# Reciprocal of the attention denominators by ln and exp on ACT, and a new order of the late units

## The chip, the cores and the metric

The kernel runs on one core of a Trainium2 chip. The metric is the device time of one execution in microseconds (us). Engines are named as in the profile: PE (matrix multiply; PEld is its weight load), DVE (vector), ACT (activation functions and copies), POOL (general), SP (which here issues all DMAs). A core has an on-chip memory, SBUF, and an accumulator memory, PSUM, into which PE writes.

## The reference

Two independent heads are computed and laid side by side in the output. S = 2048, D = 576, inputs in bf16.

```python
# A: a short convolution of k, times v, then a long convolution over the sequence (by FFT), times q
k_shift = sum over t of k_pad[:, t:t + S, :] * shift_k[:, ks - 1 - t]        # ks = 4
kv = k_shift * v
y = irfft2(rfft2(kv padded to 2S) * rfft2(ssm_k padded to 2S))[:, :S, :]
a = q * (y + kv * ssm_D)
# B: linear attention, H = 32 heads of 18
q, k, v = split(x @ wqkv)
phi = lambda t: where(t > 0, t + 1, exp(t)) + 1e-6
pq, pk = phi(q), phi(k)
kv = einsum("bhsd,bhse->bhde", pk, v);  z = einsum("bhsd->bhd", pk)
num = einsum("bhqd,bhde->bhqe", pq, kv)
den = einsum("bhqd,bhd->bhq", pq, z)[..., None] + 1e-6
b = (num / den) reshaped @ wo
out = concatenate([a, b], axis=-1)
```

## The kernel before

Part A computes the long convolution as a Fourier transform on PE, in five chunks of channels (four of 128, one of 64; chunk 4 is the small one). For each chunk ci: `cv` is the short convolution on DVE or POOL, four stages on the tile at, the last one times v; `h1` and `u1` are the first transform stage of the filter and of the data (eight matmuls of G, evicted to tiles Ch and Cu); `ht` and `ut` are DMA transposes of Ch and Cu, issued by SP, into Cth and Ctu; `h2` and `u2` are the second stage, evicted to T and SU, in two halves with two planes each; `pX`, `pT`, `pS` and `pA` are products and sums of SU and T in SBUF (an "N" in their place skips a sum, and the inverse transform then does one plane of matmuls more); `i1` is the first inverse stage, evicted to V; `i2` the second, whose eviction on DVE multiplies by q (L608). `st` stores.

Part B: `k`, `q` and `qt` make phi (an Exp on ACT, then DVE); `G`, `zs`, `zz`, `kv` and `M` make the matrix of the heads (V weights wv, x, then the output weights wo, joined into B['M'] in the tile wo_M) and the sums of pk; `den` makes the denominators of all positions and heads, 128 partitions x 512, in one PSUM tile den_ps, and their reciprocal rden, which lies in the tile Gz; `bc` (four chunks) and `bt` spread rden by matmuls over the channels, and DVE multiplies pqT and pq4 by it (L753, L762); `o` and `ol` multiply by M and store. No `o` can start before all `bc` and `bt` are done.

The order of all work is written out in a table of 296 units, ORDER, read from left to right; every engine executes its share in that order. A unit is a name with its arguments (chunk, half or plane), a letter for the engine (A ACT, D DVE, P POOL, N none), and behind the slash the places that it takes in rings of SBUF tiles and in PSUM. PSUM has four places, 0 to 3; a matmul group waits until the group that had its place before is evicted. Ch, Cu and V share two SBUF places (c8); the transposed tiles share two.

ACT holds the tables of a set of functions. The kernel loads one for the sines at the start and one for Exp in `_sine16`.

Of the kernel before, what the change touches and what calls it, by code (L numbers as in the profile page):

```python
# [42 lines left out]
h1.2.0.1.D/0 u2.1.1.1.A/03 zs/01 ut.1.0/1 u2.1.1.0.A/2 pA.0.0.N i1.0.0.0.D/10 i1.0.0.1.A/3 i1.0.1.0.A/1 zz/2
i1.0.1.1.A/0 pX.1.1.D/0 vl.1/0 cv.2.3.DDD ht.2.0/0 pT.1.1.D u2.1.0.1.A/13 u2.1.0.0.A/2 ht.2.1/1 FT.1.T hT.3.a/02 hd.4
G.3/1 cv.3.0.D cv.3.1.DD u1.2.0.0.A/00 lwv pS.1.1.D u1.2.1.1.A/3 G.0/2 cv.3.2.DD u1.2.1.0.A/1 pX.1.0.D/1 pA.1.0.N
u1.2.0.1.A/0 G.4/3 h2.2.1.1.A/22 cv.3.3.DDD h2.2.1.0.A/1 G.2/0 cv.4.0.D i2.0.0/3 h2.2.0.0.A/02 h2.2.0.1.A/1 wom kv/0
# [1 line left out]
i1.1.1.0.A/0 u2.2.0.1.A/3 pT.1.0.D cv.4.1.DD den/2 u2.2.1.1.A/11 pS.1.0.N i1.1.0.1.A/0 i1.1.0.0.A/3 lwo M.3.A/1 M.2.A/0
i2.1.1/3 u2.2.1.0.A/1 i2.1.0/0 ht.3.1/1 h2.3.1.1.A/12 hT.4.p/02 u1.3.1.1.A/01 bc.2/32 u1.3.0.1.A/0 u1.3.0.0.A/1 bt/3
M.1.A/0 u1.3.1.0.A/2 h2.3.1.0.D/1 ht.3.0/0 h2.3.0.1.A/33 bc.0/02 st.0 ut.3.0/1 h1.4.1.0.A/11 h1.4.0.1.A/3 h1.4.1.1.A/1  # L50
h2.3.0.0.A/0 bc.3/31 pX.2.0.P/0 pT.2.0.P M.4.A/2 ut.3.1/0 pX.2.1.P/1 h1.4.0.0.A/0 M.0.A/3 bc.1/20 pA.2.0.N pT.2.1.D
pS.2.1.D u2.3.0.0.A/01 u2.3.0.1.A/3 pS.2.0.P cv.4.2.PD cv.4.3.DDD i1.2.0.1.A/02 i1.2.0.0.A/1 ht.4.0/1 pX.3.0.D/0 ql.1/1
o.1.2.AAf/03 pA.2.1.P i1.2.1.1.A/2 o.0.2.AA/10 u1.4.0.0.D/13 i1.2.1.0.D/2 u1.4.1.0.A/1 h2.4.0.1.A/03 u1.4.1.1.D/0
u1.4.0.1.A/1 u2.3.1.1.A/12 u2.3.1.0.A/3 ut.4.0/0 pT.3.0.D h2.4.0.0.A/0 i2.2.1/1 pX.3.1.D/1 pA.3.1.D pS.3.0.D pA.3.0.P
o.1.0.AA/23 pT.3.1.D o.0.0.AAf/10 u2.4.0.0.A/02 u2.4.0.1.D/3 i1.3.0.1.A/11 i2.2.0/0 i1.3.0.0.A/2 st.1 pX.4.0.D/0
pT.4.0.D pA.4.0.D pS.3.1.P i1.3.1.0.A/3 pS.4.0.D i1.3.1.1.A/1 o.1.3.AAs/02 i2.3.0/3 i1.4.0.0.A/01 i1.4.0.1.D/0 i2.3.1/2
# [196 lines left out]
def kernel(  # L253
# [469 lines left out]
    def b_den():  # L723
        ps = psum.tile([128, 1024], FP32, name="den_ps")
        for c in range(4):
            for j in range(4):
# [12 lines left out]
        nc.vector.tensor_scalar_add(out=ez[:], in0=ps[:, 512:513], scalar1=EPS)
# [1 line left out]
        nc.vector.tensor_scalar(out=den, in0=den, scalar1=ez[:, 0:1], scalar2=None, op0=ALU.add)
        with nc.allow_low_precision(reason="the reciprocal is used as bf16"):
            nc.vector.reciprocal(out=B['rden'], in_=den)
# [151 lines left out]
```

## Time and profile before

| | |
|---|---|
| median of three runs | 158.18 us (158.04 to 158.29) |
| the profiled execution | 159.33 us, span of its instructions 157.6 us |
| mean granted PE clock | 0.989 |
| busy: PE, DVE, ACT, POOL | 149.6, 135.8, 130.5, 62.0 us |
| DVE's add of ez to den_ps, reciprocal of den_ps | 0.76 and 3.36 us |
| largest waits of PE in the trace | 1.1 (start), 0.5, 0.4, 0.4, 0.3 us |

How to read it: a row of a timeline gives start, duration, engine, line, operation, tile written and tiles read, how many instructions are merged, and in brackets the idle time of the engine before it and what ended that. A row of a group gives the busy total and the mean in ns of one instruction, then idle time before. In a table by stretches, "x" counts the instructions and PEclk is the share of PE's full clock that was granted. Times are us from the span's start.

### The profile page before, as it was taken

Reading aid. Unit: us, or ns where it says so; the run is one execution under the profiler, and the core shown is the slowest. Engines: PE = TensorE matmul, PEld = TensorE weight load, DVE = VectorE, ACT = ScalarE, POOL = GpSimd, SP = SyncE. Lnnn points to the kernel's source line nnn. Section 1 sums busy time; section 2 is a strip of 40 time slices with the busy share of each in tenths; the row PEclk is TensorE's granted clock in tenths of the full one; section 3 lists DMA queues with packets and bytes.
Section 4 is the critical chain, followed back from the end, with each engine's and each line's share of the span. In section 5 each row is a group of like instructions: output and inputs, shape, how many; then the busy total and the mean of one; then the engine's idle time right before and its main releaser. Section 6 shows DMA issues by size and latency. Waiting matters only on the chain.

```text
span 157.6 us, 4600 instructions
## 1 busy us (share of the span) xinstructions
PE 149.6 (95%) x1986; PEld 90.3 (57%) x1986; DVE 135.8 (86%) x169; ACT 130.5 (83%) x162; POOL 62.0 (39%) x70
## 2 busy tenths in 40 slices
PE   7999999999998999999999999999899999999991
PEld 2686555467533467367566468585445565578650
DVE  6989779898999699997999998999998998899810
ACT  4999999999987899959999757998997969796141
POOL 6048703709113963008100049289998050230000
PEclk9999999999999999999999999999987999999999
DMA  3986999999999699999999787697987999636076
GB/s 86 391 282 188 294 300 186 253 290 266 184 186 225 127 317 264 143 213 324 177 176 176 209 109 144 192 141 146 263 170 148 131 319 186 173 107 189 0 227 198
DMA packets 74315, 31.92 MB, mean 203 GB/s; under 512 B 52090, under 2 KB 73653, under 8 KB 74294
## 3 DMA queue, kind: packets, MB, share of 16 engines
q1 hardware_dynamic: 74294, 31.62, 91.5%
q8 instruction: 15, 0.25, 0.6%
q14 instruction: 6, 0.05, 0.1%
HBM read 14.97 MB, written 4.72 MB: 125 GB/s over the span
## 4 chain that ended last, share of the span: by engine, by line
PE 77%; ACT 12%; DMA 3%; DVE 3%; issue 1%; POOL 1%; DVEq 0%; POOLq 0%; ACTq 0%
PE k_ps L455 12%; PE g_ps L661 10%; PE o_ps L783 9%; PE s_ps L536 8%; PE q_ps L464 8%; PE i_ps L593 6%; PE s_ps L559 5%; DMA Ctu<-Cu 3%; PE i_ps L606 3%; PE i_ps L607 2%; ACT V L308 2%; ACT T L308 2%; ACT Cu L308 2%; PE o_ps L775 2%; ACT G L231 2%; PE qt_ps L472 2%
## 5 line engine op out<-in xcount | busy, mean ns | idle before, releaser
L455 PE MATMUL k_ps<-wqk,xT 128*128 128x512 bf16 (+1 forms) x160 | 21.5, 286 | 0.0
L536 PEld LDWEIGHTS <-G 128*128 128x128 bf16 x320 | 17.4, 98 | 3.6 <-issue 2.7
L464 PE MATMUL q_ps<-xT,wqk 128*128 128x512 bf16 x80 | 18.4, 380 | 0.0
L308 ACT ACTIVATE Cu<-s_ps 128x1024 bf16<-128x1024 f32 (+1 forms) x18 | 17.0, 976 | 0.4 <-PE s_ps L536 0.2
L455 PEld LDWEIGHTS <-xT 128*128 128x128 bf16 x160 | 11.4, 98 | 10.5 <-issue 0.3
L308 ACT ACTIVATE T<-s_ps 128x1024 bf16<-128x1024 f32 x17 | 16.8, 1026 | 0.6 <-PE s_ps L559 0.6
L308 ACT ACTIVATE ob<-o_ps 128x576 bf16<-128x576 f32 (+1 forms) x15 | 9.2, 637 | 9.1 <-PE o_ps L775 4.8
L661 PE MATMUL g_ps<-pk,x_sb 128*128 128x512 bf16 (+1 forms) x128 | 16.5, 286 | 0.0
L308 ACT ACTIVATE Ch<-s_ps 128x1024 bf16<-128x1024 f32 (+1 forms) x17 | 15.2, 928 | 1.0 <-PE s_ps L536 1.0
L494 DVE TENSOR_TENSOR at<-at 128x2048 bf16<-128x2048 bf16 (+1 forms) x14 | 15.5, 1109 | 0.5
L308 ACT ACTIVATE SU<-s_ps 128x1024 bf16<-128x1024 f32 x15 | 15.0, 1040 | 1.0 <-PE s_ps L559 1.0
L308 ACT ACTIVATE V<-i_ps 128x1024 bf16<-128x1024 f32 x15 | 14.7, 1039 | 1.0 <-PE i_ps L593 1.0
L783 PE MATMUL o_ps<-wo_M,pqT 128*128 128x512 bf16 (+1 forms) x112 | 14.9, 286 | 0.0
L448 DVE SCALAR_TENSOR_TENSOR pk<-pk,k_ps 128x576 bf16<-128x576 bf16 x16 | 11.8, 751 | 3.4 <-ACT pk L447 3.3
L493 DVE TENSOR_TENSOR at<-k,Wj 128x2048 bf16<-128x2048 bf16 (+1 forms) x13 | 14.7, 1134 | 0.1
L661 PEld LDWEIGHTS <-x_sb 128*128 128x128 bf16 x128 | 8.4, 97 | 8.9 <-issue 1.2
L447 ACT ACTIVATE pk<-k_ps,neg 128x576 bf16<-128x576 f32 x16 | 11.6, 741 | 1.3 <-PE k_ps L455 0.9
L464 PEld LDWEIGHTS <-wqk 128*128 128x128 bf16 x80 | 7.4, 98 | 9.1 <-issue 1.3
L608 DVE TENSOR_TENSOR q<-i_ps,q 128x1024 bf16<-128x1024 f32 (+1 forms) x10 | 10.9, 1105 | 1.9 <-PE i_ps L607 1.8
L783 PEld LDWEIGHTS <-pqT 128*128 128x128 bf16 x112 | 7.5, 98 | 7.7 <-issue 0.9
L536 PE MATMUL s_ps<-hT,G 128*128 128x128 bf16 (+1 forms) x160 | 10.7, 216 | 1.0 <-ACT G L231 0.4
L593 PE MATMUL i_ps<-W,T 64*128 64x128 bf16 x160 | 11.3, 217 | 0.4 <-DVE pqT L753 0.4
(163 smaller groups left out, 336.0 us busy)
## 6 DMA issues: line engine op xcount, KB each, us to landing
x_sb<-in_B_x_dram SPq DMA_DIRECT2D x4, 576.0 KB, 6.6
h_sb<-in_A_ssm_k_dram SPq DMA_DIRECT2D x4, 512.0 KB, 6.1
out_dram<-ob SPq DMA_DIRECT2D x7, 288.0 KB, 5.3
k<-in_A_k_dram SPq DMA_DIRECT2D x1, 1280.0 KB
v<-in_A_v_dram SPq DMA_DIRECT2D x1, 1280.0 KB
q<-in_A_q_dram SPq DMA_DIRECT2D x1, 1280.0 KB
wqk<-in_B_wqkv_dram SPq DMA_DIRECT2D x2, 576.0 KB, 7.8
k<-in_A_k_dram SPq DMA_DIRECT2D x1, 1024.0 KB
```

The source lines that it names most:

```text
L308: nc.scalar.activation(out=out, in_=in_, func=ACT.Copy)
L447: nc.scalar.activation(out=out_ap, in_=ps_ap, func=ACT.Exp, bias=K.neg1[0:n, :])
L448: nc.vector.scalar_tensor_tensor(out=out_ap, in0=out_ap, scalar=1.0, in1=ps_ap, op0=ALU.min, op1=ALU.max)
L455: nc.tensor.matmul(ps[:, n0:n1], lhsT=xT[r // 4][:, t, rr * 128:(rr + 1) * 128], rhs=wqk[:, t, D + n0:D + n1], start=(t == 0), stop=(t == 4))
L464: nc.tensor.matmul(ps[:, j, :], lhsT=wqk[:, t, 128 * c:128 * c + 128], rhs=xT[g][:, t, :], start=(t == 0), stop=(t == 4))
L493: on[0].tensor_tensor(out=t_, in0=kk[:, 3 - stage:19 - stage], in1=wb(stage), op=ALU.mult)
L494: on[1].tensor_tensor(out=a_, in0=a_, in1=t_, op=ALU.add)
L536: nc.tensor.matmul(ps[:, bi, 0:dc], lhsT=K.G[ri][:, b, :], rhs=xf(b), start=True, stop=True)
L593: nc.tensor.matmul(ps[:, r, g, :], lhsT=s[key, hf][64 * r:64 * r + 64, z, x, 128 * g:128 * g + 128], rhs=K.W[64 * r:64 * r + 64, m, :], st ...
L608: nc.vector.tensor_tensor(out=qs, in0=ps[:, :, 0:dc], in1=qs, op=ALU.mult)
L661: nc.tensor.matmul(ps[:, n0:n1], lhsT=x_sb[:, r, f0:f0 + fn], rhs=pk[:, r, n0:n1], start=(r == 0), stop=(r == 15))
L783: nc.tensor.matmul(pss[i][:, n0:n1], lhsT=pqT[:, c, r * 128:(r + 1) * 128], rhs=B['M'][:, c, n0:n1], start=(c == 0 and not first), stop=(c ...
```

## The change

The reciprocal is made on ACT: ln of (den + ez), with ez as the bias, written back to PSUM, and then exp of its negative. For that, the set of functions loaded in `_sine16` is the one with both ln and exp. From the 137th unit on the table differs: a few units there in engine or place, and from about the 175th on in order too.

```diff
@@ ORDER, two of its lines @@
-ut.2.0/1 i2.0.1/3 h1.3.0.0.A/12 h1.3.1.0.A/1 h1.3.0.1.D/0 h1.3.1.1.A/3 pA.1.1.P ut.2.1/0 u2.2.0.0.D/02 i1.1.1.1.A/01
+u1.3.0.0.A/2 bt/3 h1.4.1.0.A/10 u1.3.0.1.A/1 h2.3.1.0.D/2 pT.2.0.P u1.3.1.0.A/0 h2.3.0.1.A/33 bc.0/12 M.1.A/0 ut.3.0/1
...
@@ _sine16 @@
     nc.scalar.activation(out=K.sm[:, 1536:1984], in_=K.wi, func=ACT.Sin, scale=TWO_PI / 16, bias=K.negpi[:])
+    nc.scalar.preload_act_table_set("natural_log_exp_and_others")
     nc.scalar.activation(out=K.warm[:], in_=K.neg1[:], func=ACT.Exp)
@@ b_den @@
         nc.vector.tensor_scalar_add(out=ez[:], in0=ps[:, 512:513], scalar1=EPS)
         den = ps[:, 0:512]
-        nc.vector.tensor_scalar(out=den, in0=den, scalar1=ez[:, 0:1], scalar2=None, op0=ALU.add)
-        with nc.allow_low_precision(reason="the reciprocal is used as bf16"):
-            nc.vector.reciprocal(out=B['rden'], in_=den)
+        nc.scalar.activation(out=den, in_=den, func=ACT.Ln, bias=ez[:, 0:1])
+        nc.scalar.activation(out=B['rden'], in_=den, func=ACT.Exp, scale=-1.0)
```

Lines between the two edits have a number higher by one in the changed kernel. At den, DVE's order before is this (ez and den_ps are the denominators, i_ps are groups of the inverse transform, s_ps of the forward one):

```order
L310 CAST SU<-s_ps 128x2x512
L573 TENSOR_TENSOR T<-SU,T 128x2048
L493 TENSOR_TENSOR at<-k,Wj 128x16x64
L494 TENSOR_TENSOR at<-at 128x16x64
L739 TENSOR_SCALAR ez<-den_ps 128x1
L741 TENSOR_SCALAR den_ps<-den_ps,ez 128x512
L743 RECIPROCAL Gz<-den_ps 128x512
L608 TENSOR_TENSOR q<-i_ps,q 128x8x128 x2
L753 SCALAR_TENSOR_TENSOR pqT<-pqT,bc_ps 128x1024 x2
L762 SCALAR_TENSOR_TENSOR pq_77<-pq_77,bt_ps 128x1024
L310 CAST T<-s_ps 128x2x512
L753 SCALAR_TENSOR_TENSOR pqT<-pqT,bc_ps 128x1024 x6
```

and in the changed kernel, DVE, from ez on:

```order
L740 TENSOR_SCALAR ez<-den_ps 128x1
L311 CAST SU<-s_ps 128x2x512
L311 CAST V<-i_ps 128x8x32x4
L572 TENSOR_TENSOR X<-SU,T 128x2048
L609 TENSOR_TENSOR q<-i_ps,q 128x8x128 x2
L753 SCALAR_TENSOR_TENSOR pqT<-pqT,bc_ps 128x1024 x2
L762 SCALAR_TENSOR_TENSOR pq_77<-pq_77,bt_ps 128x1024
L311 CAST T<-s_ps 128x2x512
L753 SCALAR_TENSOR_TENSOR pqT<-pqT,bc_ps 128x1024 x2
L311 CAST Ch<-s_ps 128x2x16x16
L753 SCALAR_TENSOR_TENSOR pqT<-pqT,bc_ps 128x1024 x4
```

The addition and the reciprocal are gone; an SU cast, a V cast, a product X and a small Ch cast have come between ez and the last product. Ahead of ez in the changed kernel stand a T cast, the two products of chunk 0 with q, a Ch cast, the masks of kv, a product and a subtraction on T, and one conv step.

ACT at the same place, before:

```order
L308 ACTIVATE Ch<-s_ps 128x2x32x16 x3
L308 ACTIVATE V<-i_ps 128x8x32x4 x2
L308 ACTIVATE SU<-s_ps 128x2x512 x2
L308 ACTIVATE V<-i_ps 128x8x32x4 x2
L308 ACTIVATE wo_M<-m_ps 128x576 x2
```

and in the changed kernel, ACT:

```order
L309 ACTIVATE Ch<-s_ps 128x2x32x16
L309 ACTIVATE V<-i_ps 128x8x32x4 x2
L742 ACTIVATE den_ps<-den_ps,ez 128x512
L743 ACTIVATE Gz<-den_ps 128x512
L309 ACTIVATE V<-i_ps 128x8x32x4
L309 ACTIVATE SU<-s_ps 128x2x512
L309 ACTIVATE wo_M<-m_ps 128x576 x2
```

ln (L742) and exp (L743) stand behind two V casts, and behind them one V cast where two stood.

SP, at the loads of wo (numbers tell the two transposes of one Cu apart), before:

```order
L634 DMA wv_GT_1084<-in_B_wqkv_dram 64x576 x2
L543 DMA_TRANSPOSE Ctu_1656<-Cu_1397 128x16x128
L543 DMA_TRANSPOSE Ctu_1718<-Cu_1397 128x16x128
L646 DMA wo_M_1619<-in_B_wo_dram 126x4x576
L647 DMA wo_M_1619<-in_B_wo_dram 72x576
```

and in the changed kernel, SP:

```order
L635 DMA wv_GT_1085<-in_B_wqkv_dram 64x576 x2
L544 DMA_TRANSPOSE Ctu_1543<-Cu_1398 128x16x128
L647 DMA wo_M_1592<-in_B_wo_dram 126x4x576
L648 DMA wo_M_1592<-in_B_wo_dram 72x576
L544 DMA_TRANSPOSE Ctu_1664<-Cu_1398 128x16x128
```

The loads of wo, which wait for a memset of wo_M on POOL, have moved ahead of the second transpose. On POOL, behind that memset, the changed kernel has the copy of hp, two conv steps of chunk 4, the product T and the sum on X of chunk 2's half 0, the product X of its half 1, two more conv steps, and two sums; before, it had a sum on X, the copy, a product X, a product T, another product X, a sum, one conv step and three sums.

More of the change, by code (lines that the diff above doesn't have):

```diff
@@ L42 @@
 h1.2.1.1.A/1 cv.2.1.DD pT.0.0.P hd.3 pS.0.0.D q.1.1/3 h2.1.0.0.A/32 h2.1.0.1.A/0 G.1/1 cv.2.2.DP h1.2.0.0.A/2 pA.0.1.N
[L43 to L46, printed above, removed]
@@ L47 @@
-ut.2.0/1 i2.0.1/3 h1.3.0.0.A/12 h1.3.1.0.A/1 h1.3.0.1.D/0 h1.3.1.1.A/3 pA.1.1.P ut.2.1/0 u2.2.0.0.D/02 i1.1.1.1.A/01
[L48 to L56, printed above, removed]
@@ L57 @@
-o.0.3.DAs/31 i2.4.0/0 i2.4.1/2 st.2 o.1.1.AA/31 ol.0.1/023
+h1.2.0.1.A/0 u2.1.1.1.D/03 zs/01 ut.1.0/1 u2.1.1.0.A/2 pA.0.0.N i1.0.0.0.D/13 i1.0.0.1.A/0 i1.0.1.0.A/1 zz/2
+i1.0.1.1.A/3 pX.1.1.D/0 pA.1.1.N vl.1/0 cv.2.3.DDD ht.2.0/0 pT.1.1.D u2.1.0.1.A/10 u2.1.0.0.A/2 ht.2.1/1 FT.1.T
+hT.3.a/02 hd.4 G.3/1 cv.3.0.D cv.3.1.DD u1.2.0.0.A/03 lwv pS.1.1.D u1.2.1.1.A/0 G.0/2 cv.3.2.DD u1.2.1.0.A/1 pX.1.0.D/1
+pA.1.0.N u1.2.0.1.A/3 G.4/0 h2.2.1.1.A/22 cv.3.3.DDD h2.2.1.0.A/1 ut.2.0/1 G.2/3 h2.2.0.0.D/00 wom lwo i2.0.1/2
@@ new lines @@
+h2.2.0.1.A/1 u2.2.0.0.A/03 i2.0.0/0 h1.3.0.1.D/11 ut.2.1/0 h1.3.0.0.A/2 h1.3.1.0.A/3 kv/0 u2.2.0.1.A/2 h1.3.1.1.A/1
+pT.1.0.D pS.1.0.D i1.1.1.1.A/03 hT.4.p/01 i1.1.1.0.A/0 cv.4.0.D den/2 cv.4.1.PP ht.3.1/1 u2.2.1.1.D/11 i1.1.0.1.D/3
+i1.1.0.0.A/0 pX.2.0.D/0 u2.2.1.0.A/1 M.2.A/2 i2.1.0/3 i2.1.1/0 M.3.A/1 ht.3.0/0 h2.3.1.1.A/12 bc.2/31 st.0 u1.3.1.1.A/00
+u1.3.0.0.A/2 bt/3 h1.4.1.0.A/10 u1.3.0.1.A/1 h2.3.1.0.D/2 pT.2.0.P u1.3.1.0.A/0 h2.3.0.1.A/33 bc.0/12 M.1.A/0 ut.3.0/1
+h1.4.1.1.D/1 h1.4.0.1.A/3 h2.3.0.0.A/0 bc.3/23 pS.2.0.N h1.4.0.0.A/1 M.0.A/0 ut.3.1/0 pA.2.0.P M.4.A/1 bc.1/20
@@ new lines @@
+u2.3.0.0.A/03 u2.3.0.1.A/1 i1.2.0.0.A/02 ht.4.0/1 ql.1/1 i1.2.0.1.A/3 o.1.2.AAf/01 pX.2.1.P/1 pT.2.1.D pA.2.1.D pS.2.1.D
+i1.2.1.0.A/2 cv.4.2.PP cv.4.3.DDD pX.3.0.D/0 pA.3.0.P i1.2.1.1.A/3 o.0.2.AD/01 u1.4.0.1.D/12 u1.4.0.0.A/3 u1.4.1.1.A/0
+u1.4.1.0.A/1 h2.4.0.1.D/03 u2.3.1.1.A/12 i2.2.1/0 u2.3.1.0.A/1 pT.3.0.D h2.4.0.0.A/3 ut.4.0/0 pX.3.1.D/1 o.1.0.AA/20
+o.0.0.AAf/13 pS.3.0.D i1.3.0.1.A/12 pT.3.1.D pS.3.1.P pA.3.1.D u2.4.0.1.D/00 u2.4.0.0.A/1 i2.2.0/3 st.1 i1.3.0.0.A/2
+i1.3.1.1.A/0 i1.3.1.0.A/1 pX.4.0.D/0 o.1.3.AAs/32 pT.4.0.D pA.4.0.D pS.4.0.D i2.3.0/0 i1.4.0.0.A/01 i1.4.0.1.A/3
@@ L58 @@
+i2.3.1/2 o.0.3.AAs/01 i2.4.1/3 i2.4.0/2 st.2 o.1.1.AD/01 ol.0.1/320
 """
```

## The prediction

> **What bounds the kernel now.** I read the page first: span, busy shares, granted clock, the chain that ended last.
>
> ```profile
> span 157.6 us, 4600 instructions
> ...
> PE 149.6 (95%) x1986; PEld 90.3 (57%) x1986; DVE 135.8 (86%) x169; ACT 130.5 (83%) x162; POOL 62.0 (39%) x70
> PEclk9999999999999999999999999999987999999999
> PE 77%; ACT 12%; DMA 3%; DVE 3%; issue 1%; POOL 1%; DVEq 0%; POOLq 0%; ACTq 0%
> ```
>
> PE is busy for 149.6 of 157.6 us and carries 77% of the chain. The diff leaves the number of matmuls alone (five additions on T and X are skipped, "N", before and after, and each costs the inverse transform one more plane), so only PE's idle time and its lost clock can be won. The second view is therefore the table by stretches, cut where the order starts to matter: 92.9 is the end of the last long matmul group of the G stage, 109 to 121.9 is the division by the denominators, 154.1 is PE's end.
>
> ```profile
> core 0: us, PE busy (x) PEld busy (x) DVE busy (x) ACT busy (x) POOL busy (x), PEclk, DMA share, GB/s
> 92.90:109.00 16.10, 15.69 (x331) 11.72 (x329) 14.98 (x23) 13.78 (x16) 12.69 (x5) 1.00 0.76 142
> 109.00:121.90 12.90, 11.53 (x169) 6.17 (x168) 12.10 (x12) 11.71 (x16) 12.38 (x5) 0.87 0.90 196
> 121.90:132.00 10.10, 9.86 (x168) 6.01 (x162) 9.14 (x11) 8.44 (x13) 2.13 (x1) 1.00 1.06 236
> 132.00:154.10 22.10, 22.06 (x314) 13.66 (x311) 16.73 (x18) 13.56 (x19) 2.13 (x1) 1.00 0.55 137
> ```
>
> PE idles 0.41, 1.37, 0.24 and 0.04 us in the four: 2.06 us in all. In the second it also ran at a mean clock of 0.87, which is 12.9 x 0.13 = 1.68 us of work lost. Together, 3.74 us is all that a new order of the late part can win; the 3.5 us from 154.1 to the end (last eviction, last store) are written the same way in both. Finer stretches of the same view show where the clock went:
>
> ```profile
> 46.80:50.00 3.20, 2.68 (x20) 1.01 (x18) 3.17 (x4) 3.00 (x4) 0.07 (x1) 1.00 1.24 225
> ...
> 113.50:116.90 3.40, 2.87 (x42) 1.49 (x41) 3.40 (x4) 3.40 (x6) 3.40 (x2) 0.99 0.96 208
> 116.90:120.30 3.40, 3.40 (x36) 1.23 (x34) 2.71 (x3) 2.33 (x5) 3.40 (x3) 0.51 0.98 185
> ```
>
> For 3.4 us the clock was half; the 3.4 us before had PE busy for 84%, with DVE, ACT and POOL all full. Who holds PE there is read from DVE's instructions in order of time:
>
> ```profile
> 95.83 0.99 DVE L691 TENSOR_TENSOR wo_M<-kv_ps,maskbd 126x126 bf16<-126x126 f32 x5 [0.78 <-POOL X L576]
> ...
> 102.89 0.15 DVE L739 TENSOR_SCALAR ez<-den_ps 128x1 f32<-128x1 f32 x1
> 103.15 0.76 DVE L741 TENSOR_SCALAR den_ps<-den_ps,ez 128x512 f32<-128x512 f32 x1
> 103.94 3.36 DVE L743 RECIPROCAL Gz<-den_ps 128x512 bf16<-128x512 f32 x1
> 107.22 2.29 DVE L608 TENSOR_TENSOR q<-i_ps,q 128x1024 bf16<-128x1024 f32 x2
> 109.42 2.34 DVE L753 SCALAR_TENSOR_TENSOR pqT<-pqT,bc_ps 128x1024 bf16<-128x1024 bf16 x2
> 111.69 1.21 DVE L762 SCALAR_TENSOR_TENSOR pq<-pq,bt_ps 128x1024 bf16<-128x1024 bf16 x1
> 113.01 1.23 DVE L310 CAST T<-s_ps 128x1024 bf16<-128x1024 f32 x1
> 114.15 4.66 DVE L753 SCALAR_TENSOR_TENSOR pqT<-pqT,bc_ps 128x1024 bf16<-128x1024 bf16 x4
> 119.51 2.35 DVE L753 SCALAR_TENSOR_TENSOR pqT<-pqT,bc_ps 128x1024 bf16<-128x1024 bf16 x2 [0.69 <-PE bc_ps L749]
> 121.78 1.22 DVE L573 TENSOR_TENSOR T<-SU,T 128x2048 bf16<-128x2048 bf16 x1
> ```
>
> From ez at 102.89 to the last product of the division at 121.78 DVE runs with one pause, of 0.69 us, which is the half clock seen from DVE: it waits for bc matmuls that PE delivers late. The o units need all eight of these products, so DVE, not PE, bounds this stretch, and PE's 1.37 us of waiting are its shadow.
>
> **The change part by part.** Prices, one row for each kind:
>
> ```profile
> L310 DVE CAST V<-i_ps 128x1024 bf16<-128x1024 f32 x3 | 3.6, 1216 | 0.9 <-PE i_ps L593 0.9
> L571 DVE TENSOR_TENSOR X<-SU,T 128x2048 bf16<-128x2048 bf16 x7 | 8.9, 1276 | 0.2 <-ACT SU L308 0.2
> L576 DVE TENSOR_TENSOR T<-T 128x1024 bf16<-128x1024 bf16 x6 | 4.1, 684 | 0.0
> L447 ACT ACTIVATE pq<-qt_ps,neg 128x512 bf16<-128x512 f32 x2 | 1.4, 689 | 0.0
> L308 ACT ACTIVATE Ch<-s_ps 128x512 bf16<-128x512 f32 x4 | 2.3, 596 | 0.0
> L308 ACT ACTIVATE V<-i_ps 128x1024 bf16<-128x1024 f32 x15 | 14.7, 1039 | 1.0 <-PE i_ps L593 1.0
> L522 POOL COPY hp<-h_sb 64x2048 bf16<-64x2048 bf16 x1 | 3.9, 3927 | 0.0
> L573 POOL TENSOR_TENSOR T<-SU,T 128x2048 bf16<-128x2048 bf16 x2 | 8.1, 4068 | 1.6 <-DVE X L571 1.6
> L493 POOL TENSOR_TENSOR at<-k,Wj 128x1024 bf16<-128x1024 bf16 x1 | 2.1, 2138 | 0.0
> ```
>
> and, from the chain in order of time, one group of the inverse transform:
>
> ```profile
> 99.22 0.57 PE i_ps L593 x16
> ```
>
> Back to back the rows overlap: two of DVE's large instructions start 1.14 us apart, the small ones 0.6.
>
> 1. DVE loses L741 and the reciprocal: 107.22 - 103.15 = 4.07 us inside the chain. The new order fills the hole. Between ez and the last product of the division DVE has four more instructions: the casts of one SU and one V (2 x 1.14), the product X of chunk 2, half 0, which was POOL's (1.25), and a 64-column cast of Ch, which was ACT's (0.6). Sum 4.13. So the chain from ez to the end is as long as before, 18.9 us, or 18.2 us if the 0.69 us pause does not come again. This is the heart of the forecast: the reciprocal's time isn't taken off the chain, it is spent on work of ACT and POOL.
>
> 2. The chain's start. Before den, PE does the same units in another order, but the two i1 units of chunk 1, half 1, now lose their addition and take 24 matmuls instead of 16 each: 16 more, 0.57 us by the last row; the waits in that stretch, 0.41 us, mostly go, because the masks of kv at 95.83 no longer stand ahead of a product and a cast of DVE that hold PSUM. DVE itself has less ahead of ez: an SU cast (1.14) goes behind it and two conv steps (0.6 each) to POOL, a T cast (1.14) and a subtraction (0.6) are new, and the 0.78 us idle at 95.83 is covered: 1.4 us less. So ez comes when den's matmuls end, between 102.4 and 102.7 instead of 102.89: 0.2 to 0.5 us won.
>
> 3. ln and exp. No row shows ln. The nearest, an Exp of 128x512 from PSUM with a bias, took 0.69 us, a copy of that size 0.60; two that depend on each other make 1.2 to 1.4 us, and I take 1.3. The result is there at about 104.1 instead of 107.3, and that by itself wins nothing: PE reaches the first bc near 108 in both. ACT gives a T and a V cast (1.0 each) and a Ch of 64 columns (0.6) to DVE, and swaps one SU for another, so even with ln and exp it carries 1.3 us less, beside idle time of 2.3 and 1.2 us in the first two stretches. New is ACT's wait for ez: behind it stand a V cast, whose matmuls end near 104, and an SU. If ez were late, each 1 us would hold two PSUM places and cost PE up to 1 us. The changed program has the same two loads of function tables as before and none at den. Cost: 0.
>
> 4. POOL loses one product and three sums, and gets three halves of conv steps and one other sum; in its order: hp copy 3.9 from 93.5, conv 2.1 + 2.1 (the second once its DVE operand is there, 102), T of chunk 2 4.1 after X at 106.4, X addition 2.2 to 112.7, the other X 4.1 to 116.8, conv 4.3 to 121. The first readers, i1 at 119.7 and the chunk-2 products at 120.7, leave 4 us; the last conv is read at about 123: 2 us. Cost 0; with that cover gone, microsecond for microsecond on the u1 units behind it.
>
> 5. SP now issues both loads of wo ahead of the second transpose of Cu. Before:
>
> ```profile
> 94.40 1.45 SPq L543 DMA_TRANSPOSE Ctu<-Cu  x1
> 95.90 1.35 SPq L646 DMA_DIRECT2D wo_M<-in_B_wo_dram  x1
> 97.29 0.48 SPq L647 DMA_DIRECT2D wo_M<-in_B_wo_dram  x1
> ...
> DMA to landing us min/median/max: 4.3/4.9/5.4
> ```
>
> The loads wait for POOL's memset, which needs the end of the G matmuls (93.5), and take 1.35 + 0.48: the transpose is issued at 95.4 instead of 94.4 and lands by 100.8. Its reader comes after den, at 102.5, and the V cast that overwrites Cu at about 100.8. Cost 0 to 0.2; I take 0, cover 1.7 us for the reader, none for the cast.
>
> 6. Later, 121.9 to 132 held 0.24 us of PE waits around the chunk-4 casts; the new order puts i2 of chunk 2 between them, and by the rows I see no new wait: 0.2 won. Behind 132 there is nothing to win (0.04).
>
> Sum: lower end 0.2 (start) + 0 (chain) + 0.2 = 0.4; upper end 0.5 + 0.7 + 0.2 = 1.4. They differ by the pause of the half clock. The bc stretch keeps about 1.5 us of PE waits in 12 by my reckoning, as before, so I see no reason for either end and take 0.9. The profiled execution took 159.33 us (span 157.6 and 1.7 around it), 1.15 above the median of 158.18; I take the 0.9 off each, so 157.3 for the median.
>
> **One rule weighed.** In the trace the half clock came after 3.4 us with only 0.53 us of PE idle in them, while 46.8 to 50.0, equally busy, was at full clock and no drop followed. The Trainium skill, "TensorE: Matmul & The Clock Gate", Part 1, says that the clock halves after an idle window of about 3.4 us and counsels against PE gaps longer than that. By that rule neither kernel would ever slow down in mid-run; the trace disagrees, 3.4 us at 0.51, though the length of the stretch agrees with the page's window.
>
> **The rivals.**
> - Full clock throughout. Mechanism: the changed order fills the stretch that came before the drop a little better (it needs more than 84%), so PE is never slowed. Then the 1.68 us of lost work return as far as DVE lets them: 0.7 us by the chain, and up to 0.8 more if PE's earlier work lets den, and with it ez, start earlier. Gain 1.5 to 2.3, 156.3. For it: 46.8 to 50.0 stayed at full clock. Against: the same bc matmuls behind the same full DVE. By the rule of the Trainium skill's page on the clock gate, named above, this would be the forecast.
> - Nothing to measure. The chain is as long as before and ez no earlier, since den still waits on PE; 0 to 0.3, 158.0. For it: item 1, 4.07 out and 4.13 in.
> - Slower: a second half-clock stretch. PE's waits now lie spread from 109 to 120, so two successive stretches of 3.4 us can be as empty as the one that set it off. Each costs 1.68 us of PE work, of which 0.7 at least reaches the chain. From the low end of the sum that is 158.18 - 0.4 + 1.2 = 159.0 (1.2 the middle of 0.7 and 1.68). It decides from 0.9 us of further loss. Against it: one such stretch in 157.6 us so far.
>
> **How the numbers follow.** This kernel's three runs lie within 0.16%, so I count 0.2% (0.32 us) as the least that can be told from no change. Chances: the forecast (gain 0.4 to 1.4, 156.8 to 157.8) 0.51; full clock 0.15; nothing 0.20; slower 0.14. Faster is 0.66, same 0.20, slower 0.14. The range goes from the full-clock case, 156.3, to 158.8, inside the slower one: about 0.07 lies below and 0.09 above.
>
> **What would show it.** Right: DVE's rows from ez to the last product of L753 without a reciprocal, still 18 to 19 us long, ez at 102.4 to 102.7; ln and exp 0.6 to 0.7 us each at about 103 and no third table load; PE's idle time from 92.9 to its end still 1.5 to 2 us; PE's end near 153.2. Wrong: a DVE chain shorter than 17.5 us or a granted clock of 1.00 from 105 to 125 (then faster than I say), or two drops of the clock; a PE wait for the transposed Cu; ACT idle before ln for over 0.5 us; o units waiting for POOL.

## The result, and the profile after

| | changed kernel | before |
|---|---|---|
| median, 22 runs each on one chip | 157.81 us | 158.89 us |
| ratio, 95% interval | 0.9935 [0.9915, 0.9955] | |
| profiled execution, its span | 157.79 us, 156.1 us | 159.33 us, 157.6 us |

Faster by 0.65%, or 1.03 us (0.72 to 1.35) of 158.9. Some executions of most kernels here take 1.5% or more longer than the fastest of the same kernel; the medians count them, the ratios leave them out. Ratios below are against the kernel before in the same manner, and a difference "to the changed kernel" is the difference of two such ratios times 159 us. By the intervals it is good to some 0.6 to 0.7 us, and to some 0.9 to 1.0 us in experiments 2, 3 and 8, which have six runs each.

The page of the changed kernel, the lines that stand in the prediction for before:

```profile
span 156.1 us, 4608 instructions
PE 148.3 (95%) x1986; PEld 90.6 (58%) x1986; DVE 134.2 (86%) x169; ACT 130.8 (84%) x162; POOL 60.3 (39%) x70
PEclk9999999999999999999999999999999999999999
```

PE and DVE are as full as before, and the clock row has no dip. The table by stretches, cut at nearly the same places of the program (1 to 2 us earlier from the second cut on), and a finer cut of the second stretch:

```profile
core 0: us, PE busy (x) PEld busy (x) DVE busy (x) ACT busy (x) POOL busy (x), PEclk, DMA share, GB/s
92.90:108.00 15.10, 14.92 (x323) 11.40 (x316) 13.88 (x23) 12.48 (x15) 10.35 (x5) 1.00 0.86 165
108.00:120.90 12.90, 11.45 (x186) 6.95 (x183) 12.86 (x13) 12.11 (x16) 12.70 (x5) 1.00 0.77 173
120.90:130.00 9.10, 8.94 (x155) 5.71 (x149) 7.88 (x10) 8.11 (x12) 2.12 (x1) 1.00 1.17 254
130.00:152.60 22.60, 22.41 (x328) 13.88 (x319) 16.75 (x18) 15.05 (x21) 2.44 (x1) 1.00 0.51 136
...
116.80:120.20 3.40, 2.85 (x48) 1.50 (x49) 3.40 (x4) 2.82 (x5) 3.32 (x2) 1.00 1.04 194
```

PE idles 0.18 + 1.45 + 0.16 + 0.19 = 1.98 us, against 2.06 before. The granted clock is 1.00 in every stretch, also behind one (116.80 to 120.20) in which PE was busy for only 84%. DVE in order of time, from ez to behind the last product of the division:

```profile
102.48 0.16 DVE L740 TENSOR_SCALAR ez<-den_ps 128x1 f32<-128x1 f32 x1 [0.17 <-PE den_ps L737]
102.75 1.22 DVE L311 CAST SU<-s_ps 128x1024 bf16<-128x1024 f32 x1
103.89 1.22 DVE L311 CAST V<-i_ps 128x1024 bf16<-128x1024 f32 x1
105.02 1.22 DVE L572 TENSOR_TENSOR X<-SU,T 128x2048 bf16<-128x2048 bf16 x1
106.32 2.35 DVE L609 TENSOR_TENSOR q<-i_ps,q 128x1024 bf16<-128x1024 f32 x2
...
116.14 4.60 DVE L753 SCALAR_TENSOR_TENSOR pqT<-pqT,bc_ps 128x1024 bf16<-128x1024 bf16 x4
120.66 1.22 DVE L574 TENSOR_TENSOR T<-SU,T 128x2048 bf16<-128x2048 bf16 x1
```

There is no reciprocal and no pause: 120.66 - 102.48 = 18.18 us. ACT at den, and SP at the loads of wo:

```profile
102.73 0.66 ACT L742 ACTIVATE den_ps<-den_ps,ez 128x512 f32<-128x512 f32 x1
103.43 0.60 ACT L743 ACTIVATE Gz<-den_ps 128x512 bf16<-128x512 f32 x1
...
92.86 0.35 SPq L647 DMA_DIRECT2D wo_M<-in_B_wo_dram  x1
93.25 0.45 SPq L648 DMA_DIRECT2D wo_M<-in_B_wo_dram  x1
94.58 3.29 SPq L544 DMA_TRANSPOSE Ctu<-Cu  x1
```

ln takes 0.66 us and exp 0.60, with no idle time in front of ln; the transpose is issued at 94.58, where it was 94.40.

**Where the time went.** Three rows of PE mark the same points in every kernel here: the start of the last long G group, the first `o` group, and the last `o` group. In the changed kernel:

```profile
88.71 4.12 PE L662 MATMUL g_ps<-pk,x_sb 128*128 128x512 bf16 x32
...
121.00 0.46 PE L775 MATMUL o_ps<-wo_M,pq 64*128 64x512 bf16 x4
...
152.25 0.29 PE L802 MATMUL o_ps<-wo_M,pq 64*128 64x288 bf16 x1
```

The same differences for the traces of experiments 1 to 7 (us):

| kernel | start of G group | G group to first o | first o to last o |
|---|---|---|---|
| before, first profile (with half clock) | 88.77 | 33.35 | 31.64 |
| before, second profile | 89.01 | 32.61 | 31.65 |
| changed | 88.71 | 32.29 | 31.25 |
| ln and exp in the old order | 90.00 | 36.30 | 31.63 |
| new order, reciprocal on DVE | 88.68 | 37.20 | 31.19 |
| conv step back on DVE | 88.00 | 33.36 | 31.20 |
| shorter DVE chain | 88.62 | 32.16 | 31.28 |
| shorter DVE chain, T cast on DVE | 89.98 | 32.42 | 31.80 |
| new order up to the division, sum on POOL | 89.45 | 32.29 | 32.68 |
| new order up to the division, sum on DVE | 89.32 | 32.29 | 31.67 |

The first column moves by 2 us from one execution to the next. Up to the first matmul of G (at 65.79, 66.05 and 65.75 us in the first three traces) the table of units is the same in both kernels, and from there to the marked row each of the three takes 22.96 to 22.98 us. So the first column is the noise of a single trace, and the other two are nearly free of it. At full clock the new order wins 0.32 us between G and the division and 0.40 us behind it, 0.72 us together, the lower end of what the runs measured. The rest, 0.3 us, is not located: the first column differs by as much (89.01 - 88.71), but it does so ahead of any difference in the table, by noise.

The 0.40 us behind the division is not idle time by the profile's count. From the first `o` to PE's end PE idles 0.24 us in before and 0.29 us after; with 471 matmul records each, its busy time falls from 31.69 to 31.25 us. The rows of PE that differ most are those of `u1` of chunk 4 (32 matmuls, which read v and G) and of the second stage of chunks 3 and 4 (which read Cth and Ctu), first in before, then in the changed kernel:

```profile
127.53 0.41 PE L536 MATMUL s_ps<-v,G 128*128 128x64 bf16 x8
...
128.42 0.41 PE L536 MATMUL s_ps<-v,G 128*128 128x64 bf16 x8
...
129.10 0.85 PE L536 MATMUL s_ps<-v,G 128*128 128x64 bf16 x16
129.88 0.41 PE L559 MATMUL s_ps<-Ctu,W 64*32 64x512 bf16 x8
130.47 0.41 PE L559 MATMUL s_ps<-Ctu,W 64*32 64x512 bf16 x8 [0.18 <-ACT T L308]
```

```profile
126.88 0.64 PE L537 MATMUL s_ps<-v,G 128*128 128x64 bf16 x16
127.68 0.63 PE L537 MATMUL s_ps<-v,G 128*128 128x64 bf16 x16 [0.16 <-ACT ob L309]
128.25 0.41 PE L560 MATMUL s_ps<-Cth,W 64*32 64x512 bf16 x8
...
129.81 0.41 PE L560 MATMUL s_ps<-Ctu,W 64*32 64x512 bf16 x8
```

The durations can't be added up: a row runs on past the start of the next (127.53 + 0.41 is 127.94, and PE's next row starts at 127.86), and a short wait can hide in that. So the time is counted from the start of each matmul to the start of the next, waits included, from the first `o` to the last (us):

| matmuls of | before | changed | experiment 7, sum on DVE (old order here) |
|---|---|---|---|
| `o` | 19.23 | 19.08 | 19.25 |
| second stage (`h2`, `u2`) | 2.05 | 1.67 | 2.05 |
| `u1` | 1.46 | 1.37 | 1.46 |
| `i1` and `i2` | 8.91 | 9.12 | 8.91 |

The largest part, 0.38 us, is the second stage. In before, PE waits there for a cast of T on ACT (0.18 us in the row at 130.47), and in the changed kernel `i2` of chunk 2 stands in this place. The rest fits with fewer changes from one kind of matmul to another, 18 in place of 21: most of them take 0.12 to 0.15 us from start to start, where the matmuls within a unit of `u1` are 0.03 us apart. The old order puts other units between the four of `u1`; the new one runs them in a row, in two pairs.

### The profile page after: what moved, and what is told of

It is laid out like the page before. It is cut to its first block, busy times and chain, and to the rows that moved or that the text cites. A ratio compares the mean times of both kernels' runs of the same rounds, so it can differ in the third digit from the quotient of the medians.

```text
span 156.1 us, 4608 instructions
## 1 busy us (share of the span) xinstructions
PE 148.3 (95%) x1986; PEld 90.6 (58%) x1986; DVE 134.2 (86%) x169; ACT 130.8 (84%) x162; POOL 60.3 (39%) x70
## 4 chain that ended last, share of the span: by engine, by line
PE 62%; DMA 12%; ACT 11%; DVE 8%; issue 2%; POOLq 2%; POOL 1%; SPq 1%; DVEq 0%; ACTq 0%
PE k_ps L456 10%; PE g_ps L662 10%; PE s_ps L537 8%; PE q_ps L465 6%; DMA q<-in_A_q_dram 6%; PE i_ps L594 5%; PE s_ps L560 4%; PE o_ps L783 4%; DMA Cth<-Ch 3%; DMA Ctu<-Cu 3%; DVE q L609 2%; DVE pqT L753 2%; PE i_ps L607 2%; PE i_ps L608 2%; ACT G L231 2%
## 5 line engine op out<-in xcount | busy, mean ns | idle before, releaser
L465 PE MATMUL q_ps<-xT,wqk 128*128 128x512 bf16 x80 | 18.4, 380 | 0.0
L309 ACT ACTIVATE V<-i_ps 128x1024 bf16<-128x1024 f32 x16 | 15.5, 1025 | 1.1 <-PE i_ps L594 0.8
L309 ACT ACTIVATE Ch<-s_ps 128x1024 bf16<-128x1024 f32 (+1 forms) x17 | 15.7, 952 | 0.3 <-PE s_ps L537 0.3
L309 ACT ACTIVATE T<-s_ps 128x1024 bf16<-128x1024 f32 x15 | 14.8, 1026 | 0.8 <-PE s_ps L560 0.7
L495 DVE TENSOR_TENSOR at<-at 128x2048 bf16<-128x2048 bf16 (+1 forms) x12 | 14.2, 1181 | 0.9 <-POOL at L494 0.4
L309 ACT ACTIVATE SU<-s_ps 128x1024 bf16<-128x1024 f32 x14 | 14.1, 1027 | 0.7 <-PE s_ps L560 0.6
L494 DVE TENSOR_TENSOR at<-k,Wj 128x2048 bf16<-128x2048 bf16 (+1 forms) x12 | 14.1, 1171 | 0.0
L495 POOL TENSOR_TENSOR at<-at 128x1024 bf16<-128x1024 bf16 (+1 forms) x3 | 8.3, 2772 | 14.0 <-DVE at L494 10.9
```

Of the source, the lines that this page charges most:

```text
L309: nc.scalar.activation(out=out, in_=in_, func=ACT.Copy)
L465: nc.tensor.matmul(ps[:, j, :], lhsT=wqk[:, t, 128 * c:128 * c + 128], rhs=xT[g][:, t, :], start=(t == 0), stop=(t == 4))
L494: on[0].tensor_tensor(out=t_, in0=kk[:, 3 - stage:19 - stage], in1=wb(stage), op=ALU.mult)
L495: on[1].tensor_tensor(out=a_, in0=a_, in1=t_, op=ALU.add)
```

## The experiments

**1. Was the half clock part of it? The kernel before, profiled again (no edit).**

> The kernel before, unchanged, for a second profile. In 20 of its 23 timed runs the mean clock was 0.995 or more, 0.989 in three, so this profile should show the full clock around 115 to 121. My theory (the half clock of the first profile was part of the price of the old order): its span is then 0.5 to 0.7 us shorter than 157.6, DVE's chain from ez to the last product of the division takes 18.2 us instead of 18.9, and the changed kernel's lead shrinks to 0.4 to 0.7 us. Rival (the half clock cost next to nothing, the order itself costs 1 us): span within 0.3 us of 157.6 and PE waits of 2.5 to 3 us from 92 to 132.

158.82 us, span 157.1, granted clock 1.0. Its DVE chain:

```profile
103.13 0.15 DVE L739 TENSOR_SCALAR ez<-den_ps 128x1 f32<-128x1 f32 x1
...
114.41 6.95 DVE L753 SCALAR_TENSOR_TENSOR pqT<-pqT,bc_ps 128x1024 bf16<-128x1024 bf16 x6
121.27 1.43 DVE L573 TENSOR_TENSOR T<-SU,T 128x2048 bf16<-128x2048 bf16 x1
```

Six products back to back, and 121.27 - 103.13 = 18.14 us, as expected. So the pause of 0.69 us is there in the trace with the half clock and not in the one without. G to first o is 0.74 us shorter than in the first profile, and the span 0.5 us; the changed kernel's span of 156.1 us is still 1.0 us ahead, where 0.4 to 0.7 was expected. A mean clock of 0.989, the mark of one such stretch, occurred in 3 of 23 runs of the kernel before on one chip, in 2 of 17 and 1 of 23 on two others, and in none of the 22 of the changed kernel. With 6 of 63 runs it has next to no part in the medians.

**2. ln and exp alone, in the order of before.**

```diff
 (before, its ORDER unchanged)
+    nc.scalar.preload_act_table_set("natural_log_exp_and_others")
-        tensor_scalar(den + ez); reciprocal on DVE
+        activation(Ln, bias=ez); activation(Exp, scale=-1.0) on ACT
```

> The order of before, with ln and exp on ACT in place of DVE's addition and reciprocal. My theory (the freed time is worth only what the new order puts into it): on ACT ln has to wait for ez at 102.9 and stands with exp (1.3 us) ahead of the casts whose V the next inverse transform needs, so that this reaches PE at about 107 instead of 105.6; DVE's first product of the division comes no earlier than the 109.4 of before. Time 0 to 1.5 us above before, likeliest +0.7. Rival (DVE bounds the stretch, so 4.07 us off DVE is a gain by itself, in any order): PE's 1.4 us of waits and the half clock's 1.7 us both go, 1.5 to 3 us below before.

161.7 us median, ratio 1.0138 [1.0082, 1.0194]: 2.2 us slower than before. ACT, and DVE's next instruction behind ez (at 104.14), in the trace, which is of the slowest of the six executions (163.47 us, mean clock 0.974) and 1.23 us later at G than the first trace of before:

```profile
105.57 1.02 ACT L309 ACTIVATE SU<-s_ps 128x1024 bf16<-128x1024 f32 x1
106.47 1.95 ACT L309 ACTIVATE V<-i_ps 128x1024 bf16<-128x1024 f32 x2
...
109.56 2.56 DVE L609 TENSOR_TENSOR q<-i_ps,q 128x1024 bf16<-128x1024 f32 x2 [5.28 <-PE i_ps L608]
```

The 4 us that DVE is spared lie there as 5.28 us of idle time. ln and exp stand ahead of an SU and two V casts on ACT; those V casts end 18.4 us behind the start of the G group, in before 16.7 (at 105.5), PE's i2 units wait for them, and DVE's product with q for i2, which starts 1.1 us later than before when counted in the same way. In this trace G to first o is 3.7 us longer than in the second profile of before: 1.7 of that stand by 117, where the third of the eight products starts, and the other 2.0 come behind it, where the clock was at 0.87, 0.50 and 0.63 in three stretches of 3.4 us from 116.8 on. The three executions with a mean clock of 0.998 or more took 160.21, 160.38 and 162.00 us, so there is a loss without the half clock too. The rival, by which the chain gets shorter by what is taken out, is refuted, and the loss is larger than expected.

**3. The new order alone, with the reciprocal on DVE.**

```diff
 (changed kernel, its ORDER unchanged)
-    nc.scalar.preload_act_table_set("natural_log_exp_and_others")
-        activation(Ln, bias=ez); activation(Exp, scale=-1.0) on ACT
+        tensor_scalar(den + ez); reciprocal on DVE
```

> The new order with the addition and the reciprocal on DVE as before. My theory (DVE's chain from ez to the last product of the division sets when the o units start): the chain is 18.2 us in the changed kernel and becomes 22.2; the o units start near 125 instead of 121.0, PE waits 3.5 to 4 us more, time 3 to 4 us above the changed kernel, 2 to 3 above before. Rival (the gain came from PE's clock and the order of PE's units, DVE has slack): less than 1 us above the changed kernel.

164.62 us, ratio 1.0376 [1.0318, 1.0434]: 7 us above the changed kernel. Its largest wait of PE, two stretches, and DVE's one pause between ez and the last product:

```profile
PE s_ps L559 <- DVE SU L310: 3.9, 1, 3.9
...
103.40:106.80 3.40, 0.68 (x26) 0.59 (x19) 3.37 (x3) 1.02 (x1) 1.14 (x1) 1.00 0.39 73
106.80:110.20 3.40, 2.21 (x19) 1.22 (x19) 3.39 (x4) 1.49 (x2) 0.00 (x0) 0.58 0.10 20
...
111.20 2.35 DVE L608 TENSOR_TENSOR q<-i_ps,q 128x1024 bf16<-128x1024 f32 x2 [1.00 <-PE i_ps L607]
```

The SU cast behind the reciprocal holds a PSUM place for 3.9 us more, PE has nothing to do, and the clock halves; all six runs have a mean clock of 0.976 to 0.990. G to first o is 37.20 us, 4.9 more than in the changed kernel: the 4 us of the reciprocal, which were expected, and the pause of 1.0 us, in which DVE waits for matmuls made at the half clock, which was not. The profiled execution is the fastest of the six (162.61 us). The other 2 us of the median lie in executions of which there is no trace, three of them with a mean clock of 0.976, and stay open. The rival, less than 1 us, is refuted.

**4. Is DVE's chain the bound? Add to it: a conv step back from POOL to DVE.**

```diff
-cv.4.1.PP
+cv.4.1.DD
```

> The changed kernel with the conv step of chunk 4 behind den (two instructions of 0.6 us) on DVE instead of POOL, so that they stand between ez and the last product of the division. My theory: the chain is 1.25 us longer, o starts 1.2 us later, time 0.8 to 1.3 us above the changed kernel. Rival (the chain has slack; the half clock made the difference): 0 to 0.3 us.

158.76 us, ratio 0.9996 [0.9963, 1.0028]: 0.97 us above the changed kernel, as the theory said (0.8 to 1.3). The two instructions stand behind ez, and PE pays:

```profile
101.84 0.68 DVE L494 TENSOR_TENSOR at<-k,Wj 128x1024 bf16<-128x1024 bf16 x1
102.56 0.69 DVE L495 TENSOR_TENSOR at<-at 128x1024 bf16<-128x1024 bf16 x1
...
PE s_ps L560 <- DVE SU L311: 1.0, 1, 1.0
```

The chain is 19.25 us, 1.07 longer, and G to first o is longer by 33.36 - 32.29 = 1.07 us. What is added goes to the end in full. This one edit takes back the whole gain.

**5. Take from it: products of two chunks on half the columns.**

```diff
+            w = 1 if c in (0, 2) else 2
-            p = pqT[:, c, ...]
+            p = pqT[:, c, ...][:, 0:w, :]
```

> The changed kernel, but the products of chunks 0 and 2 of the division (four of eight) are made on half of their columns only, so half of those channels stay undivided; the matmuls are all there. DVE's chain is 4 x 0.5 = 2.1 us shorter. My theory: o starts earlier until PE has no waits left in 108 to 121 (1.45 us there), time 0.8 to 1.4 us below the changed kernel. Rival (the chain has slack): 0 to 0.3 us below.

158.59 us, ratio 0.9942 [0.9901, 0.9983], that of the changed kernel. The freed 2.1 us come back as pauses of DVE:

```profile
110.24 1.22 DVE L763 SCALAR_TENSOR_TENSOR pq<-pq,bt_ps 128x1024 bf16<-128x1024 bf16 x1 [0.46 <-PE bt_ps L761]
111.82 1.23 DVE L311 CAST T<-s_ps 128x1024 bf16<-128x1024 f32 x1 [0.36 <-PE s_ps L560]
...
114.65 0.69 DVE L311 CAST Ch<-s_ps 128x512 bf16<-128x512 f32 x1 [0.18 <-ACT T L309]
115.90 4.62 DVE L754 SCALAR_TENSOR_TENSOR pqT<-pqT,bc_ps 128x1024 bf16<-128x1024 bf16 x4 [0.56 <-PE bc_ps L749]
```

G to first o falls by 0.13 us only. My theory that DVE alone bounds this stretch falls: a longer chain of DVE costs its full length (experiment 4), a shorter one wins next to nothing. In the stretch from 108 to 120.9 ACT was then the fuller one, 12.08 of 12.9 us against DVE's 11.20, so the next theory was that the two bind together.

**6. The same, and a T cast moved from ACT to DVE.**

```diff
-h2.3.0.1.A/33
+h2.3.0.1.D/33
```

> The changed kernel with the products of bc chunks 0 and 2 on half of their columns only (the other half of pqT isn't multiplied), which frees 2.1 us of DVE as in the run before it with that edit, and in addition one T cast of chunk 3 (1.0 us on ACT) is given to DVE (1.2 us). Theory 1 (DVE and ACT are equally full at the division and hold PE together through the four PSUM places): with both relieved by about 1 us the time falls 0.4 to 0.8 us below the changed kernel. Theory 2 (the written order of the PSUM places holds PE, whoever evicts): within 0.2 us of the kernel with the halved products, so no gain either.

158.25 us, ratio 0.9964 [0.9922, 1.0006]: no gain over experiment 5 (0.3 us above it, less than the error). The same stretch of experiment 5, then of this:

```profile
108.00:120.90 12.90, 11.30 (x185) 6.90 (x183) 11.20 (x13) 12.08 (x16) 12.60 (x5) 1.00 0.78 175
```

```profile
108.00:120.90 12.90, 11.32 (x156) 6.21 (x154) 11.93 (x13) 9.92 (x14) 12.82 (x5) 1.00 0.81 183
```

ACT falls to 9.92 us and DVE stays below the 12.86 of the changed kernel, yet PE is idle for 1.58 us here, 1.60 in experiment 5 and 1.45 in the changed kernel (this execution runs 1.3 us late at G, so the cut lies that much earlier in the program; moved along with G, the stretch has ACT at 10.90 us, DVE at 11.93 and PE idle for 1.74; G to first o, 32.42 us, says the same). Theory 1 falls too. What stays is theory 2, that the sequence of evictions in the four PSUM places holds PE whoever does them; the runs fit it, but no run changed that sequence alone, so it stays open.

**7. Which part of the order wins? The new one up to the division, the old one behind it**, first with the sum pA of chunk 2, half 1, on POOL as in the old order, then on DVE as in the new.

```diff
 (ORDER from its 244th unit on, behind bc; - changed kernel, + this one, with the sum on DVE)
-o.1.2.AAf/01 pX.2.1.P/1 pT.2.1.D pA.2.1.D pS.2.1.D i1.2.1.0.A/2 cv.4.2.PP
+pX.2.1.P/1 pT.2.1.D pA.2.1.D pS.2.1.D cv.4.2.PP cv.4.3.DDD pX.3.0.D/0 o.1.2.AAf/01
...
-u1.4.0.1.D/12 u1.4.0.0.A/3 u1.4.1.1.A/0 u1.4.1.0.A/1
+u1.4.0.0.D/11 i1.2.1.0.D/2 u1.4.1.0.A/3 h2.4.0.1.A/01 u1.4.1.1.D/0 u1.4.0.1.A/3
```

> The new order up to the end of the division (last i1 units of chunk 2, half 0), then the old order of the o units and chunks 3 and 4, with the PSUM places of the old part renamed so that they join. My theory (all but 0.2 us of the gain comes ahead of the first o unit): 0 to 0.4 us above the changed kernel. Rival (the tail was searched too and carries half the gain): 0.5 to 1 us above it.

> The new order up to the division and the old order behind it, as in the run before it with that edit, but the sum pA of chunk 2, half 1, is on DVE as in the changed kernel, so that POOL no longer adds in SBUF while DVE subtracts there. Theory 1 (the clash of the two engines cost that run its 2 us): now 0 to 0.5 us above the changed kernel, and the L578 rows of T and X of about 0.7 us on DVE without stretching. Theory 2 (the old order of the late part is itself worse by so much): still 1 to 2 us above the changed kernel.

Sum on POOL: 160.03 us, ratio 1.0064 [1.0023, 1.0104], 2.1 us above the changed kernel, a miss for the theory (0 to 0.4) and the rival (0.5 to 1) alike. Two rows of it, DVE and POOL:

```profile
122.65 2.50 DVE L578 TENSOR_TENSOR T<-T 128x1024 bf16<-128x1024 bf16 x1
...
121.47 3.13 POOL L578 TENSOR_TENSOR X<-X 128x1024 bf16<-128x1024 bf16 x1
```

That subtraction takes 0.69 us elsewhere on DVE, and that sum 2.12 on POOL; side by side they took 2.50 and 3.13. Sum on DVE: 158.47 us, ratio 0.9983 [0.9942, 1.0025], 0.8 us above the changed kernel; the subtraction and the sum, both on DVE, are 0.69 us each. G to first o is 32.29 us in both, as in the changed kernel, and first o to last o is 31.67, that of before to 0.03 us. So the clash cost 32.68 - 31.67 = 1.0 us by the traces, half of the 2 us that theory 1 gave it, and the new order behind the first o wins 0.4 us. The 0.8 us of the runs, with their error of 0.6 to 0.7, agree with that and with the expected 0 to 0.5.

**8. Could it be faster? Product X of chunk 2, half 0, back on POOL**, ahead of den, then (with conv step 2 on DVE in exchange) behind den; and each with the T cast of experiment 6 on DVE.

```diff
 (ahead of den)
+pX.2.0.P/0 cv.4.0.D den/2 cv.4.1.PP
-i1.1.0.0.A/0 pX.2.0.D/0
 (behind den)
+den/2 pX.2.0.P/0 cv.4.1.PP
-i1.1.0.0.A/0 pX.2.0.D/0
-cv.4.2.PP
+cv.4.2.DD
```

> The changed kernel with the product X of chunk 2, half 0, on POOL, ahead of den, instead of DVE behind ez: DVE's chain is 1.25 us shorter, POOL has idle time of 3.0 and 1.7 us for the 4.1 us. Theory that only DVE's load bounds the division: 0.6 to 1.2 us below the changed kernel. Theory after the run with halved products (ACT and DVE bound it together through the four PSUM places, so that DVE alone wins nothing): 0 to 0.3 us below.

> As the kernel with X on POOL, and the cast of T of chunk 3, half 0 (second plane), 1.0 us, moved from ACT to DVE, so that the freed time of DVE takes load off ACT. Theory that ACT and DVE bound the division together: 0.4 to 0.9 us below the changed kernel. Theory that only DVE's load counts: 0 to 0.2 us below. Theory that neither counts but the order in which the four PSUM places come free: no change, within 0.2 us.

> The changed kernel with the product X of chunk 2, half 0, back on POOL (4.1 us), placed right behind den where DVE's next work reads PSUM (casts of SU and V, products with i_ps), and in exchange the second conv step of chunk 4 behind it on DVE (two halves of 0.6 us). Theory 1 (POOL and DVE hold each other up only where both read SBUF operands): no stretched DVE row at ez, and the time within 0.5 us of the changed kernel, 7 us below the run that had the same product on POOL ahead of den. Theory 2 (DVE's chain alone sets the end): a chain shorter by 1.25 us, so 0.6 to 1.2 us below the changed kernel. Theory 3 (POOL's product of 4.1 us is itself too slow at any place): 3 us or more above.

> As the run before (X of chunk 2, half 0, on POOL behind den), and the T cast of chunk 3, half 0, second plane, moves from ACT (1.0 us) to DVE (1.2 us), so that ACT is relieved where DVE has been. Theory 1 (ACT and DVE bind together at the division): 0.3 to 0.8 us below the changed kernel. Theory 2 (neither binds alone or together, the order of PSUM places does): within 0.3 us of the kernel without this move. What could spoil it: POOL's second product X then ends near 121 and the inverse transform of chunk 2 waits for it.

| X on POOL | median | ratio |
|---|---|---|
| ahead of den | 165.33 us | 1.0404 [1.0346, 1.0463] |
| ahead of den, T cast on DVE | 167.71 us | 1.0577 [1.0521, 1.0632] |
| behind den | 167.05 us | 1.0474 [1.0404, 1.0543] |
| behind den, T cast on DVE | 166.28 us | 1.0463 [1.0400, 1.0526] |

All four are misses by 7 us or more. DVE and POOL ahead of den, and then behind it:

```profile
100.81 4.56 DVE L577 TENSOR_TENSOR T<-T 128x1024 bf16<-128x1024 bf16 x1
105.30 2.60 DVE L492 TENSOR_TENSOR at<-k,Wj 128x1024 bf16<-128x1024 bf16 x1
...
100.77 4.06 POOL L572 TENSOR_TENSOR X<-SU,T 128x2048 bf16<-128x2048 bf16 x1 [3.61 <-ACT Ch L309]
```

```profile
103.11 4.55 DVE L577 TENSOR_TENSOR T<-T 128x1024 bf16<-128x1024 bf16 x1
...
103.06 4.05 POOL L572 TENSOR_TENSOR X<-SU,T 128x2048 bf16<-128x2048 bf16 x1 [3.60 <-ACT Ch L309]
```

A subtraction of 0.69 us and a conv step of 0.69 us on DVE take 4.56 and 2.60, the first beside POOL's product X, the second beside the conv step that POOL does next (2.57 us from 104.78): 5.8 us more, and ez comes 5.5 us late (counted from POOL's memset). G to first o is 39.16 us in this trace, 6.9 more than in the changed kernel, so 1.3 us more are lost behind ez. The third run was meant to put the product where DVE reads PSUM, and did not: `den` has no work on POOL, so a unit written behind it stands at the same place in POOL's queue, and POOL starts as soon as SU and T are there, at 103.06, with ez only at 110.11. The theory it was to test, that the product is harmless beside casts from PSUM, was not tested at this place. The first profile of before has a row that speaks for it:

```profile
102.89 4.06 POOL L571 TENSOR_TENSOR X<-SU,T 128x2048 bf16<-128x2048 bf16 x1 [3.28 <-ACT SU L308]
```

There the same product X runs on POOL beside DVE's addition and reciprocal, which read PSUM, and takes its usual 4.06 us.

## Why the prediction was right, and where it was not

The faster side was given 0.66, and the gain was put at 0.9 us; 1.03 us (0.72 to 1.35) was measured. The median came to 157.81 us where 157.3 was given, because 22 runs of the kernel before have a median of 158.89, 0.7 above that of the three runs I started from. Point by point:

- **Item 1, the chain keeps its length: right, and it is the heart of it.** 18.18 us after, 18.14 before at full clock. The order spends the reciprocal's time on casts and a product of other engines. Experiments 2 and 3 show the two halves of the change to be one: ln and exp without the order cost 2.2 us, the order without ln and exp 6.0 us, and both together win 1.
- **Item 2, ez earlier by 0.2 to 0.5 us: right.** 102.48 where I said 102.4 to 102.7, and 0.35 us earlier than before when counted from G; it waits for den's matmuls (0.17 us), as I said. At full clock, G to first o is 0.32 us shorter.
- **Item 3, ln and exp for nothing: right here.** 1.26 us where I took 1.3, no third load of tables (two of 1.28 us, as before), ln 0.1 us behind ez. Its warning, ACT's wait for ez and what is queued behind, is what experiment 2 ran into.
- **Items 4 and 5, POOL and SP at no cost: right in the sum.** No wait of PE for either. For POOL the reason I gave, time in hand before the readers, was incomplete: experiment 8 shows that it is as important what DVE does beside POOL.
- **Item 6, 0.2 us won behind the division: right in kind, too small.** It was 0.40 us. The wait for the T cast among the chunk-4 units (0.18 us) went, by `i2` of chunk 2 in its place, as I counted; but "no new wait" was wrong (0.16 us for a cast of ob came), and the fewer changes between kinds of matmul I had not counted at all. Experiment 7, with the old order of these units, has the old times of each kind and 31.67 in all.
- **The upper end, 0.7 us for the pause of the half clock: wrong.** The profiled execution of before was one of the few with a half-clock stretch. The median had none to give back, so 0.35 us of the 0.9 had no ground; item 6 and the unlocated 0.3 us stand in its place. That the size came out right is in part luck: two errors offset each other.
- **"DVE, not PE, bounds this stretch": half right.** Adding 1.07 us costs 1.07 us (experiment 4), taking 2.1 us away wins 0.13 (experiment 5). A chain without pauses shows that a longer one costs; it does not show that a shorter one wins.
- **The rule weighed.** That a drop can come without a long gap stays as the first trace showed it (0.53 us of idle time in the 3.4 us before). Experiment 3 shows a drop with a long one: PE waits for 3.9 us up to 107.99, and the granted clock is 1.00 until 107.3 and about half from there to 110.8. That is the case which the Trainium skill, "TensorE: Matmul & The Clock Gate", Part 1, describes, and the trace agrees. "Full clock throughout" described the changed kernel, but also the usual execution of before, so it was no rival and brought nothing. I had named a granted clock of 1.00 from 105 to 125 as a sign that the kernel would be faster than I said; the sign came, and the time did not. The gain of 1.5 to 2.3 us that I gave this rival does not follow from its two terms either, which make 1.5 at most (0.7 + 0.8).

## What to carry to other kernels

Work taken off an engine's chain wins nothing by itself: it wins what the order then does with the hole, so look for what moves in, and ask of the work moved elsewhere what stands behind it in the new queue. Ask in both directions of a stretch that seems bound by one engine, since one with no slack can cost when lengthened and give nothing when shortened. And before a lost clock is counted as a gain, look whether the ordinary runs lose it too; one profile is one execution.

## What the hardware showed that was not expected

- **DVE and POOL hold each other up when both read two operands from SBUF.** A subtraction on DVE took 4.56 us instead of 0.69 beside POOL's product (4.06), and another took 2.50 beside a sum on POOL that itself went from 2.12 to 3.13. Beside work of DVE that reads PSUM there is no such loss: in the changed kernel POOL's conv step from 102.45 takes its usual 2.12 us beside casts that take their usual 1.22. The Trainium skill, "SBUF — State Buffer", section "Who interferes with whom", says that a DVE instruction with two SBUF inputs contends with a GpSimd (POOL) instruction that reads SBUF, and that the one issued first holds the port for its whole length. The traces agree: 4.56 us is the time until POOL's product ends (104.83) and DVE's own half a microsecond. Here it decides which placements on POOL are free.
- **The half clock comes and goes between executions of one kernel** (3 of 23, 2 of 17 and 1 of 23 runs, mean clock 0.989), in the same program, while all six runs of experiment 3, whose trace has a wait of 3.9 us at the drop, show a mean clock of 0.976 to 0.990.
